# Two attention and two spectral layers on one core: the token transform written with real cosine and sine coefficients

## The chip, the core and the metric

The kernel runs on one core of a Trainium2 chip. The core has five engines with queues of their own that run in program order: TensorE (PE, with its weight loads as PEld), VectorE (DVE), ScalarE (ACT), GpSimd (POOL) and SyncE (SP, which here only issues DMAs). They meet through semaphores. The metric is the time of one launch on the device, in microseconds, and lower is better. Inputs and output are float32.

## The reference

```python
def _B_ref(x, w_r, w_i):
    B, S, D = x.shape                       # 1, 2048, 576
    X = rfft2(x, axes=(-2, -1))
    X = X * (w_r + 1j * w_i)                # 2048 x 289
    return irfft2(X, s=(S, D), axes=(-2, -1))

x = A_x
x = x + _A_ref(_layernorm(x), A_wqkv, A_wo)   # attention, 32 heads of 18, causal window of 256
x = x + _B_ref(_layernorm(x), B_w_r, B_w_i)   # global filter in frequency
x = x + _A_ref(_layernorm(x), A_wqkv, A_wo)
x = x + _B_ref(_layernorm(x), B_w_r, B_w_i)
return x
```

The change is in `_B_ref`: a two-dimensional real Fourier transform over 2048 tokens and 576 features, a product with a complex weight, and the way back.

## The kernel before

One program does the four layers in turn. `layer_a` is an attention layer (layer norm, projection to queries, keys and values, scores, softmax, values, output projection). At its end it calls `layer_b`, the spectral layer. Instructions run on each engine in the order in which the code lists them. No scheduler moves them, so an instruction that waits holds up everything behind it on its engine.

The 2048 tokens are written as 128 x 16: token index = 16 n1 + n2, with n2 from 0 to 15. `layer_b` has three stages, and the second and third are pipelines that `pipe` writes out: in each step t it calls every stage function once, in the listed order, for the item t minus the function's lag.

- **The f stage** handles one n2 (128 tokens) at a time. `f0` applies the layer norm and forms sums and differences of mirrored features, `f1` transposes them (PSUM tile `tp`, one buffer) and splits them into a high and a low part (`et`), `f2` does the feature transform by matmul (`pf`) and splits it (`yh`, `yl`), and `f3` does a transform over the 128 values of n1 (`pz`) with 12 matmuls, copies it to `ye` on DVE and writes it to the DRAM scratch `yd[0]`. The same loop finishes the output projection of the attention layer: `out.unit` does 28 matmuls (`ops`) and the residual, `out.sums` and `out.stats` the layer norm's statistics (L584 to L591), and `out.ahead` transposes the next rows (`tpo`, in the same PSUM buffer as `tp`) and splits them (L537 to L550). Every product is in float32r with a high and a low part.
- **The g stage** handles 16 groups of 8 frequencies. `g1m` does the transform over n2 (`p`), multiplies by the weight `w` on DVE and combines on POOL (`uv`, L302 and L303). `g2` does the inverse over n2 (`pq`) and writes to the scratch `yd[1]`. Both use plain float32 and half the array's rows or columns per matmul. It ends with the first loads of the next stage.
- **The i stage** handles one n2 at a time again, with `pipe(NT, [(0, ly), (4, i1), (5, i2), (2, i0)])`. `ly` loads one n2, `i0` splits it into a high and a low part (`z`, shown as `oroom`: ACT L346, DVE L347, ACT L348, DVE L349), `i1` does the inverse over n1 (`pi`, 18 matmuls) and splits it (`zh`, `zl`: ACT L368, DVE L369, ACT L370, DVE L371), and `i2` does the inverse feature transform (`po`, 16 matmuls) and adds the residual (ACT L389, DVE L390 and L391, POOL L392 and L393). In step t the order is thus i1 for t-4, i2 for t-5, i0 for t-2. In the first spectral layer the steps from t = 7 on also carry pieces of the next attention layer (`nxt`).

In time, the first spectral layer runs from about 475 us (with the end of the output projection) to 748 us: the f stage to 621, the g stage to 668, the i stage to 750. The second runs from 1217 us to the end: the f stage to 1361, the g stage to 1409, the i stage to 1492.

Of the kernel before, what the change touches and what calls it, by code (L numbers as in the profile page):

```python
# [16 lines left out]
DF = 289  # L17
NF = 290
# [7 lines left out]
def hl(x):  # L26
    h = r12(x)
    l = r12(np.asarray(x, np.float64) - h)
    return h.astype(np.float32), l.astype(np.float32)

def consts_b():
    n = np.arange(DF)[:, None].astype(np.int64)
    f = np.arange(DF)[None, :].astype(np.int64)
    ang = 2 * np.pi * ((n * f) % D) / D
    C = np.cos(ang)
    Sn = np.sin(ang)
    Sn[:, 0] = Sn[:, 288] = 0.0
# [22 lines left out]
    G = np.exp(-2j * np.pi * ((n1 * n1.T) % 128) / 128)  # L60

    k1 = ((2 * np.arange(4)[None, None] + np.arange(2)[:, None, None]) * 16 + np.arange(16)[None, :, None])
    def cplx(M, axis):

        return [np.stack(p, axis=axis) for p in ((M.real, M.imag), (-M.imag, M.real))]

    gc = np.zeros((128, 2, 2, 2, 128), np.float32)

    ga = np.zeros((16, 2, 4, 2, 2, 256), np.float32)
    for j in range(2):  # L70
        for c, m in enumerate(cplx(G[:, k1[j]], 3)):
            gc[:, 0, j, c], gc[:, 1, j, c] = hl(m.reshape(128, 128))
        for c, m in enumerate(cplx(G.conj()[k1[j]], 2)):
            ga[:, c, :, 0, j], ga[:, c, :, 1, j] = hl(m.reshape(16, 4, 256))
# [12 lines left out]
    return dict(dc=dc, ic=ic, fc=fc.reshape(128, 4096), gc=gc.reshape(128, 1024), ga=ga.reshape(128, 1024), m2=m2.reshape(128, 4096))

def lay_w(wr, wi):
    w = np.zeros((16, 128, 2, NF), np.float32)  # L90
    for c, a in enumerate((wr, wi)):

        b = a.reshape(16, 8, 16, DF)

        w[:, :, c, :DF] = b.reshape(16, 4, 2, 16, DF).transpose(3, 2, 1, 0, 4).reshape(16, 128, DF)
    return w.reshape(16, 128, 2 * NF)

def layer_b(tc, src, dst, dcs, gc, ident, rh, rl, out, ic_d, fc_d, ga_d, m2_d, w_d, dram, nxt, share):
# [8 lines left out]
    with ExitStack() as stack:  # L107
# [10 lines left out]
        ga = rh[:, 4248:5272].rearrange("p (a j c) -> p a j c", a=2, j=2)  # L118
        ic = rh[:, 5272:8752].rearrange("p (a f) -> p a f", f=NF)
        pairs = [rl[:, 1160 * k:1160 * k + 1160] for k in range(4)]  # L120
        yis, tws = [[rl[:, at + 580 * k:at + 580 * k + 580].rearrange("p (a f) -> p a f", f=NF) for k in range(n)] for at, n in ((4640, 4), (6960, 2))]
# [12 lines left out]
                for q in range(2):  # L134
                    xs[n2 + q] = x[:, q]

        fc = cp.tile([128, 16, 2, 2, 64], F32, name="fc")
        m2 = cp.tile([128, 16, 2, 128], F32, name="m2")
        eos = []
        for j in range(4):  # L140
            e = cp.tile([128, 2, 290], F32, name=f"eo{j}")
# [13 lines left out]
        def pre(n2):  # L155

            if n2 in (1, 4, 7, 10):
                k = (1, 4, 7, 10).index(n2)
                nc.sync.dma_start(fc[:, 4 * k:4 * k + 4].rearrange("p g j c m -> p (g j c m)"), fc_d[:, 1024 * k:1024 * k + 1024])
            if n2 in (2, 6, 9, 12):  # L160
                k = (2, 6, 9, 12).index(n2)
                nc.sync.dma_start(m2[:, 4 * k:4 * k + 4].rearrange("p g c m -> p (g c m)"), m2_d[:, 1024 * k:1024 * k + 1024])
            if n2 % 2 and n2 // 2 < NW:
                pre_w(n2 // 2)

# [43 lines left out]
        def f3(n2, h):  # L209
            pz = pp.tile([128, 2, 512], F32, tag="mm", name=f"pz{n2}", bufs=3)  # L210
            yh, yl = h["yh"], h["yl"]
            for j in range(2):
                ms = [(t, c, y) for c in range(2) for t, y in ((0, yh), (0, yl), (1, yh))]
                for k, (t, c, y) in enumerate(ms):
                    T.matmul(pz[:, j, 0:NF], gc[:, t, j, c], y[:, c], start=k == 0, stop=k == 5)  # L215
# [73 lines left out]
        def g1m(g, h):  # L289
            ps = pp.tile([128, 2, 512], F32, tag="mm", name=f"p2_{g}", bufs=3)  # L290

            for c in range(2):
                for j in range(2):
                    T.matmul(ps[64 * j:64 * j + 64, c, 0:NF], fc[:, g, j, c], h["y"][:, j], start=True, stop=True)  # L294
# [3 lines left out]
            V.tensor_mul(p1, ps[:, :, 0:NF], w)  # L298
# [3 lines left out]
            P.tensor_sub(uv[:, 0], p1[:, 0], p1[:, 1])  # L302
            P.tensor_add(uv[:, 1], p2[:, 0], p2[:, 1])  # L303
# [3 lines left out]
        def g2(g, h):  # L307
# [2 lines left out]

            for c in range(2):
                for j in range(2):
                    T.matmul(pq[:, j, 0:NF], m2[64 * j:64 * j + 64, g, c], uv[64 * j:64 * j + 64, c], start=c == 0, stop=c == 1)  # L313
# [29 lines left out]
        def i0(n2, h):  # L343
            z = zs[n2 % 3]
            zf = z.bitcast(F32)
            A.copy(z[:, 0, :, 0:DF], h["y"][:, :, 0:DF])  # L346
            V.tensor_sub(z[:, 1, :, 0:DF], h["y"][:, :, 0:DF], zf[:, 0, :, 0:DF])  # L347
            A.copy(z[:, 0, :, 320:353], zf[:, 0, :, 256:289])  # L348
            V.tensor_copy(z[:, 1, :, 320:353], zf[:, 1, :, 256:289])  # L349

        def i1(n2, h):
# [2 lines left out]
            psf = ps.rearrange("p a b -> p (a b)")  # L354
            for ch in range(3):
                lo, m = ((0, 128), (128, 128), (256, 97))[ch]
                o = psf[0:m, ch * 256:ch * 256 + 256]
                k = 0
                for c in range(2):
                    for sl, mo in ((0, ga[:, 0, c]), (0, ga[:, 1, c]), (1, ga[:, 0, c])):  # L360
                        T.matmul(o, z[:, sl, c, lo:lo + m], mo, start=k == 0, stop=k == 5)  # L361
# [115 lines left out]
class Out:  # L477
# [6 lines left out]
    def room(self):  # L484
# [5 lines left out]
        self.gc = rh[:, 9216:10240].rearrange("p (a j b c) -> p a j b c", a=2, j=2, b=2)  # L490
# [18 lines left out]
    def consts(self):  # L509

        self.dcs = []
        for k, t in enumerate(("wraw", "wraw", "wqh", "wqh", "wql")):
            d = self.bp.tile([128, 2, NF], F32R, tag=t, name=f"dc{k}", bufs=2)
            self.nc.sync.dma_start(d.bitcast(F32), self.dc_d[:, 2 * k:2 * k + 2].bitcast(F32))
            self.dcs.append(d)
        self.nc.sync.dma_start(self.gc.rearrange("p a j b c -> p (a j b c)").bitcast(F32), self.gc_d.bitcast(F32))

    def load(self, u):
        self.nc.sync.dma_start(self.o[u % 3], self.ov[:, u])
# [673 lines left out]
```

## Time and profile before

| | us |
|---|---|
| median of 3 runs (1497.03, 1502.33, 1503.27) | 1502.33 |
| the profiled execution's own time | 1494.12 |
| its span in the profile | 1492.4 |
| PE busy in the span | 1428.8 |
| DVE busy | 941.7 |
| ACT busy | 811.4 |
| POOL busy | 686.1 |

The busy time of PE counts pipelined matmuls whose ends are modelled, so two matmuls that follow each other overlap in it. In rows of the timeline the first two numbers are the start and the duration in microseconds, and a bracket at the end tells how long the engine had been idle and what it waited for. The start-to-start spacing of two rows on an engine is what one of them costs there. The windows view gives, for a stretch of time, its length and then the busy time of PE, PEld, DVE, ACT and POOL with the number of instructions, the granted TensorE clock as a share of full speed, the DMA share and GB/s.

### The profile page before, as it was taken

The numbers are of one execution on the slowest core, as the hardware profiler recorded it, in microseconds if no ns is written. First come the engines' busy times: TensorE is split into PE (matmuls) and PEld (weight loads), VectorE is DVE, ScalarE is ACT, GpSimd is POOL, SyncE is SP. The second block draws the span as 40 slices with busy tenths as digits, with TensorE's granted clock in tenths as the row PEclk, the third lists the DMA queues.
The fourth block names the chain that finished last, engine by engine and source line by source line (L and its number), as shares of the span: only waits on it lengthen the run. The fifth ranks groups of instructions, "written<-read, shape, count | busy, mean of one in ns | idle before, by whom it ended". The sixth has DMA issues, their size and how long they took to land.

```text
span 1492.4 us, 34861 instructions
## 1 busy us (share of the span) xinstructions
PE 1428.8 (96%) x12124; PEld 1091.4 (73%) x12124; DVE 941.7 (63%) x3090; ACT 811.4 (54%) x1962; POOL 686.1 (46%) x1124
## 2 busy tenths in 40 slices
PE   7999999999998899999999999999999988999997
PEld 7976666666656799759999756666665568997697
DVE  5328777777882655456852388777777735554476
ACT  5524777777785444224454257777777754442243
POOL 2266455555565432153421954555454644332434
PEclk9999999999999999999999999999999999999999
DMA  6656556565445465767663575555554354667663
GB/s 194 198 171 215 170 180 190 180 188 176 155 131 162 129 216 183 241 209 247 240 173 92 184 219 169 168 159 166 158 149 144 102 173 142 210 198 248 215 206 124
DMA packets 203241, 267.66 MB, mean 179 GB/s; under 512 B 103938, under 2 KB 109058, under 8 KB 202106
## 3 DMA queue, kind: packets, MB, share of 16 engines
q1 hardware_dynamic: 192890, 242.75, 52.9%
q10 hardware_dynamic: 7808, 15.62, 3.0%
q0 software_dynamic: 2368, 7.05, 1.7%
q8 instruction: 97, 1.59, 0.4%
q14 instruction: 78, 0.64, 0.1%
HBM read 166.71 MB, written 102.00 MB: 180 GB/s over the span
## 4 chain that ended last, share of the span: by engine, by line
PE 70%; DVE 6%; DMA 6%; ACT 5%; POOL 3%; issue 2%; SPq 1%; ACTq 0%; POOLq 0%; DVEq 0%
PE pj L798 16%; PE S L855 11%; PE U L912 10%; PE ops L555 6%; PE E L892 5%; PE vps L738 4%; PE pf L202 3%; PE pz L215 3%; PE pi L361 2%; DMA ofree<-yd 2%; PE tpo L926 2%; PE po L382 2%; ACT P L893 2%; PE pq L313 1%; PE p L294 1%
## 5 line engine op out<-in xcount | busy, mean ns | idle before, releaser
L857 DVE CUSTOM_DVE_ANT_0 jk<-S,mask 128x384 bf16<-128x384 f32 (+2 forms) x1024 | 490.6, 529 | 112.1 <-PE E L892 61.6
L893 ACT ACTIVATE P<-E 128x384 f32<-128x384 f32 (+2 forms) x1024 | 409.2, 476 | 124.0 <-PE E L892 104.2
L895 POOL TENSOR_SCALAR_AFFINE_SELECT P<-P 128x512 f32<-128x512 f32 x256 | 163.1, 637 | 276.7 <-ACT P L893 254.7
L855 PE MATMUL S<-ks,qs 63*128 63x384 f32 (+2 forms) x1024 | 269.7, 372 | 1.1 <-issue 0.4
L892 PE MATMUL E<-qs,ks 64*128 64x384 f32 (+2 forms) x1024 | 222.5, 373 | 5.5 <-ACT P L893 3.7
L855 PEld LDWEIGHTS S<-ks,qs 63*128 63x128 f32 x1024 | 140.9, 185 | 105.7 <-DVE m L857 73.7
L912 PE MATMUL U<-P,vq 128*19 128x128 f32 (+1 forms) x3840 | 188.5, 329 | 1.0 <-ACT us L917 1.0
L798 PE MATMUL pj<-xh,wqh 128*128 128x512 f32 x360 | 156.1, 433 | 2.9 <-ACT vt L742 1.7
L912 PEld LDWEIGHTS U<-P,vq 128*19 128x19 f32 x3840 | 95.8, 98 | 77.9 <-issue 21.4
L898 POOL TENSOR_SCALAR_AFFINE_SELECT P<-P 128x512 f32<-128x512 f32 x224 | 142.8, 637 | 0.0
L892 PEld LDWEIGHTS E<-qs,ks 64*128 64x128 f32 x1024 | 114.1, 185 | 19.8 <-ACT P L893 10.9
L555 PE MATMUL ops<-oroom 128*128 128x288 f32 x840 | 120.8, 299 | 4.4 <-DVE oroom L538 3.0
L798 PE MATMUL pj<-xh,wql 128*128 128x512 f32 x360 | 124.5, 419 | 0.4 <-POOL wql L460 0.4
L798 PE MATMUL pj<-xl,wqh 128*128 128x512 f32 x288 | 121.6, 422 | 0.0
L555 PEld LDWEIGHTS ops<-oroom 128*128 128x128 f32 x840 | 112.8, 189 | 6.2 <-DVE oroom L538 3.9
L171 POOL TENSOR_TENSOR eo<-xn 128x287 f32<-128x287 f32 x32 | 26.1, 816 | 153.7 <-ACT xn L169 127.0
L798 PEld LDWEIGHTS pj<-xh,wqh 128*128 128x128 f32 x360 | 67.6, 188 | 34.2 <-issue 10.4
L813 DVE TENSOR_TENSOR sg<-pj,sg 128x512 fp32r<-128x512 f32 x72 | 49.5, 687 | 58.3 <-ACT sg L810 58.2
L857 DVE DVE_READ_ACCUMULATOR2_ANT m<- 128x1 f32 x1024 | 85.1, 83 | 0.0
L361 PE MATMUL pi<-oroom 128*128 128x256 f32 (+1 forms) x576 | 77.4, 289 | 5.0 <-ACT oroom L346 3.8
L798 PEld LDWEIGHTS pj<-xh,wql 128*128 128x128 f32 x360 | 64.2, 189 | 21.0 <-issue 10.7
L361 PEld LDWEIGHTS pi<-oroom 128*128 128x128 f32 (+1 forms) x576 | 72.8, 186 | 6.9 <-ACT oroom L346 4.8
(179 smaller groups left out, 2626.6 us busy)
## 6 DMA issues: line engine op xcount, KB each, us to landing
qk_d<-sg SPq DMA_DIRECT2D x56, 512.0 KB
qs<-qk_d SPq DMA_DIRECT2D x384, 72.0 KB
ks<-qk_d SPq DMA_DIRECT2D x348, 72.0 KB
v_d<-vt SPq DMA_DIRECT2D x32, 304.0 KB
vq<-v_d SPq DMA_DIRECT2D x16, 608.0 KB
yd<-ye SPq DMA_DIRECT2D x32, 290.0 KB
wt<-in_w SPq DMA_DIRECT2D x16, 580.0 KB
x<-ofree SPq DMA_DIRECT2D x32, 288.0 KB
```

Source lines behind the costliest of these rows:

```text
L361: T.matmul(o, z[:, sl, c, lo:lo + m], mo, start=k == 0, stop=k == 5)
L555: self.nc.tensor.matmul(self.ps[u][n][:, 0:288], x, self.w[p][:, wk * D + n * 288:wk * D + n * 288 + 288], start=first and i == 0, stop=la ...
L738: T.matmul(ps[:, n, 0:288], xT(xk, c), w[:, wk, n * 288:(n + 1) * 288], start=i == 0, stop=i == len(ks) - 1)
L798: T.matmul(box["ps"].rearrange("r (n p) -> r n p", n=NT) if second else box["ps"], w[:, wk], x, start=s == 0, stop=s == len(ks) - 1)
L813: V.tensor_sub(rest[:, 1], by, rest[:, 0].bitcast(F32))
L855: T.matmul(ps[:, 0:N], q[b:b + 63, pair, i * 128:i * 128 + 128], k[b:b + 63, pair, lo:hi], start=True, stop=True)
L857: V.tensor_tensor_reduce(out=jk[:, 0:N], in0=ps[:, 0:N], in1=mask[:, 384 - N:384], scale=1.0, scalar=-3e38, op0=ALU.add, op1=ALU.max, accu ...
L892: T.matmul(ps[:, 0:nq], k[b:b + 64, pair, j * 128:j * 128 + 128], q[b:b + 64, pair, j * 128:j * 128 + nq], start=True, stop=True)
L893: A.activation(p[:, hl_, 0:nq], ps[:, 0:nq], AF.Exp, scale=SC)
L895: P.affine_select(out=p[:, :, 0:128], in_=p[:, :, 0:128], pattern=[[0, 4], [1, 128]], compare_op=ALU.is_ge, fill=0.0, base=0, channel_mult ...
L898: P.affine_select(out=p[:, :, 256:384], in_=p[:, :, 256:384], pattern=[[0, 4], [-1, 128]], compare_op=ALU.is_gt, fill=0.0, base=0, channel ...
L912: T.matmul(U[32 * h:32 * h + 19, (q0 % 4) * 128:(q0 % 4) * 128 + 128 * (q1 - q0)], vts[n][:, j, h], pt[n, j][:, h, (q0 - j) * 128:(q1 - j) ...
```

## The change

The transform over n1 is no longer complex. Its input is real for each of the cosine and sine parts of the features, so the coefficients over n1 are taken as cosines and sines of 64 frequencies, and a frequency k is kept together with its mirror 128 - k. The constants `gc` and `ga` are half as large, `fc` and `m2` are 17 groups instead of 16, and the rows of `w` follow the new order.

- In `f3` the 12 matmuls become 6: for j = 1 and then j = 0, three each. DVE's one copy `ye` becomes three instructions: ACT copies half of the PSUM tile to `half`, and DVE writes the sum and the difference of the other half and `half`.
- In `g1m` the group g = 0 has 8 matmuls instead of 4 (each output accumulates two), and in `g2` the 4 matmuls of group 0 contract over 128 rows instead of 64.
- In `i0` POOL first writes the sum and the difference of the two loaded halves to a new tile `both` (two buffers), and ACT's copy and DVE's subtraction read `both` in place of the loaded tile.
- In `i1` there are still 18 matmuls, but each has 128 columns instead of 256 and writes a range of its own.

```diff
         def f3(n2, h):
...
-            for j in range(2):
-                ms = [(t, c, y) for c in range(2) for t, y in ((0, yh), (0, yl), (1, yh))]
-                for k, (t, c, y) in enumerate(ms):
-                    T.matmul(pz[:, j, 0:NF], gc[:, t, j, c], y[:, c], start=k == 0, stop=k == 5)
+            for j in (1, 0):
+                for k, (t, y) in enumerate(((0, yh), (0, yl), (1, yh))):
+                    T.matmul(pz[:, j, 0:NF], gc[:, t, j], y[:, j], start=k == 0, stop=k == 2)
             ye = wp.tile([128, 2, NF], F32, tag="ye", name=f"ye{n2}", bufs=3)
-            V.tensor_copy(ye, pz[:, :, 0:NF])
+            half = ip.tile([128, 2, NF], F32, tag="both", name=f"half{n2}", bufs=2)[:, 0]
+            A.copy(half, pz[:, 1, 0:NF])
+            V.tensor_add(ye[:, 0], pz[:, 0, 0:NF], half)
+            V.tensor_sub(ye[:, 1], pz[:, 0, 0:NF], half)
...
         def g1m(g, h):
...
-                    T.matmul(ps[64 * j:64 * j + 64, c, 0:NF], fc[:, g, j, c], h["y"][:, j], start=True, stop=True)
+                    T.matmul(ps[64 * j:64 * j + 64, c, 0:NF], fc[:, g, j, c], h["y"][:, j], start=True, stop=g > 0)
+                    if g == 0:
+                        T.matmul(ps[64 * j:64 * j + 64, c, 0:NF], fc[:, 16, j, c], h["y"][:, 1 - j], start=False, stop=True)
...
         def g2(g, h):
...
-                    T.matmul(pq[:, j, 0:NF], m2[64 * j:64 * j + 64, g, c], uv[64 * j:64 * j + 64, c], start=c == 0, stop=c == 1)
+                    r = slice(64 * j, 64 * j + 64) if g else slice(0, 128)
+                    T.matmul(pq[:, j, 0:NF], m2[r, g if g or j == 0 else 16, c], uv[r, c], start=c == 0, stop=c == 1)
...
         def i0(n2, h):
             z = zs[n2 % 3]
             zf = z.bitcast(F32)
-            A.copy(z[:, 0, :, 0:DF], h["y"][:, :, 0:DF])
-            V.tensor_sub(z[:, 1, :, 0:DF], h["y"][:, :, 0:DF], zf[:, 0, :, 0:DF])
+            y = h["y"]
+            w = ip.tile([128, 2, NF], F32, tag="both", name=f"both{n2}", bufs=2)
+            P.tensor_add(w[:, 0, 0:DF], y[:, 0, 0:DF], y[:, 1, 0:DF])
+            P.tensor_sub(w[:, 1, 0:DF], y[:, 0, 0:DF], y[:, 1, 0:DF])
+            A.copy(z[:, 0, :, 0:DF], w[:, :, 0:DF])
+            V.tensor_sub(z[:, 1, :, 0:DF], w[:, :, 0:DF], zf[:, 0, :, 0:DF])
             A.copy(z[:, 0, :, 320:353], zf[:, 0, :, 256:289])
             V.tensor_copy(z[:, 1, :, 320:353], zf[:, 1, :, 256:289])
...
         def i1(n2, h):
...
-                o = psf[0:m, ch * 256:ch * 256 + 256]
-                k = 0
                 for c in range(2):
-                    for sl, mo in ((0, ga[:, 0, c]), (0, ga[:, 1, c]), (1, ga[:, 0, c])):
-                        T.matmul(o, z[:, sl, c, lo:lo + m], mo, start=k == 0, stop=k == 5)
-                        k += 1
+                    o = psf[0:m, ch * 256 + 128 * c:ch * 256 + 128 * c + 128]
+                    for k, (sl, mo) in enumerate(((0, ga[:, 0, c]), (0, ga[:, 1, c]), (1, ga[:, 0, c]))):
+                        T.matmul(o, z[:, sl, c, lo:lo + m], mo, start=k == 0, stop=k == 2)
```

The rest of the diff builds the new constants on the host (`consts_b`, `pairs_of`, `lay_w`), makes the tiles `fc`, `m2`, `gc` and `ga` fit, and loads one more group with the last pieces of `fc` and `m2`.

More of the change, by code (lines that the diff above doesn't have):

```diff
@@ L59, in consts_b @@
     n1 = np.arange(128)[:, None]
-    G = np.exp(-2j * np.pi * ((n1 * n1.T) % 128) / 128)
-    k1 = ((2 * np.arange(4)[None, None] + np.arange(2)[:, None, None]) * 16 + np.arange(16)[None, :, None])
-    def cplx(M, axis):
-        return [np.stack(p, axis=axis) for p in ((M.real, M.imag), (-M.imag, M.real))]
-    gc = np.zeros((128, 2, 2, 2, 128), np.float32)
-    ga = np.zeros((16, 2, 4, 2, 2, 256), np.float32)
-    for j in range(2):
[L71 to L74, printed above, removed]
+    m = np.arange(64)
+    wave = np.exp(2j * np.pi * ((n1 * m) % 128) / 128)
+    sign = 1.0 - 2.0 * (n1 % 2)
+    up, down = (np.concatenate([e, z[:, 1:]], axis=1) for e, z in ((np.ones((128, 1)), wave.real), (0 * sign, wave.imag)))
+    even = np.stack([up, -down], axis=2)
+    odd = np.stack([down, up], axis=2)
+    even[:, 0] = odd[:, 0] = np.concatenate([np.ones((128, 1)), sign], axis=1)
+    even, odd = [a.reshape(128, 16, 4, 2) for a in (even, odd)]
+    gc = np.zeros((128, 2, 2, 128), np.float32)
+    ga = np.zeros((16, 2, 4, 2, 2, 128), np.float32)
+    for j, a in enumerate((even, odd)):
+        gc[:, 0, j], gc[:, 1, j] = hl(a.reshape(128, 128))
+        back = a.copy()
+        back[:, 0, 0] *= 0.5
+        ga[:, :, :, 0, j], ga[:, :, :, 1, j] = hl(back.transpose(1, 3, 2, 0))
+    k1 = pairs_of()
+    def cplx(M, axis):
+        return np.stack((M.real, M.imag), axis=axis)
     fc = np.zeros((16, 4, 2, 16, 2, 2, 4, 16), np.float32)
+    fx = np.zeros((16, 4, 2, 2, 2, 4, 16), np.float32)
     m2 = np.zeros((2, 4, 16, 16, 2, 2, 4, 16), np.float32)
+    mx = np.zeros((2, 4, 16, 2, 2, 2, 4, 16), np.float32)
     for j in range(2):
@@ L91, in lay_w @@
     for c, a in enumerate((wr, wi)):
-        b = a.reshape(16, 8, 16, DF)
-        w[:, :, c, :DF] = b.reshape(16, 4, 2, 16, DF).transpose(3, 2, 1, 0, 4).reshape(16, 128, DF)
+        k = pairs_of()[..., None] + 128 * np.arange(16)
+        w[:, :, c, :DF] = a[k].transpose(1, 0, 2, 3, 4).reshape(16, 128, DF)
     return w.reshape(16, 128, 2 * NF)
@@ L135, in ld @@
                     xs[n2 + q] = x[:, q]
-        fc = cp.tile([128, 16, 2, 2, 64], F32, name="fc")
-        m2 = cp.tile([128, 16, 2, 128], F32, name="m2")
+        fc = cp.tile([128, 17, 2, 2, 64], F32, name="fc")
+        m2 = cp.tile([128, 17, 2, 128], F32, name="m2")
         eos = []
@@ L489, in room @@
         self.oL = [rh[:, 8448 + 256 * k:8704 + 256 * k] for k in range(3)]
-        self.gc = rh[:, 9216:10240].rearrange("p (a j b c) -> p a j b c", a=2, j=2, b=2)
+        self.gc = rh[:, 9216:9728].rearrange("p (a j c) -> p a j c", a=2, j=2)
         small = f[:, 8130:8170]
```

40 lines of the change are left out of this document (29 added, 11 removed).

## The prediction

> **What bounds the kernel now.** I read the engine totals first, then the busy time per stretch in the spectral stages, and then the timeline of each engine through one turn of each loop that the change touches.
>
> ```profile
> PE 1428.8 (96%) x12124; PEld 1091.4 (73%) x12124; DVE 941.7 (63%) x3090; ACT 811.4 (54%) x1962; POOL 686.1 (46%) x1124
> ```
>
> ```profile
> 1426.47:1477.80 51.33, 51.33 (x411) 51.33 (x410) 43.09 (x72) 23.52 (x60) 23.61 (x24) 1.00 0.57 186
> 519.70:587.20 67.50, 67.50 (x523) 67.50 (x521) 38.35 (x96) 28.92 (x64) 22.02 (x54) 1.00 0.63 200
> ```
>
> PE looks like the bound: it never rests in twelve turns of the second i stage (first row) or in eight turns of the first f stage (second row, 67.5 / 8 = 8.44 us each). But DVE is busy for 43.1 of 51.3 us in the i stage, and a share cannot tell whether its gaps are free. So I followed one turn there, from one residual add (DVE L390) to the next:
>
> ```profile
> 1436.21 0.46 DVE L390 TENSOR_TENSOR xo<-ofree,po 128x289 f32<-128x289 f32 x1
> 1436.58 0.45 DVE L391 TENSOR_TENSOR xo<-ofree,po 128x287 f32<-128x287 f32 x1
> 1436.95 1.22 DVE L347 TENSOR_TENSOR oroom<-ofree,oroom 128x578 fp32r<-128x578 f32 x1
> 1438.97 0.69 DVE L369 TENSOR_TENSOR zl<-pi,zh 128x512 fp32r<-128x512 f32 x1 [0.20 <-ACT zh L368]
> 1440.11 0.43 DVE L371 TENSOR_TENSOR zh<-pi,zh 33x256 fp32r<-33x256 f32 x1 [0.44 <-ACT zh L370]
> 1440.57 0.46 DVE L390 TENSOR_TENSOR xo<-ofree,po 128x289 f32<-128x289 f32 x1
> ...
> 1438.20 0.25 ACT L348 CAST oroom<-oroom 128x66 fp32r<-128x66 f32 x1 [1.61 <-DVE oroom L347]
> 1438.36 0.58 ACT L368 CAST zh<-pi 128x512 fp32r<-128x512 f32 x1
> 1439.70 0.38 ACT L370 CAST zh<-pi 97x256 fp32r<-97x256 f32 x1 [0.76 <-DVE zl L369]
> ...
> 1436.75 0.81 POOL L392 TENSOR_TENSOR xo<-xo,bs 128x289 f32<-128x289 f32 x1 [2.38 <-DVE xo L390]
> 1437.51 1.21 POOL L393 TENSOR_TENSOR xo<-xo,bs 128x287 f32<-128x287 f32 x1
> ```
>
> Each start follows the end before it: L390, L391, L347 on DVE; then ACT L348, which waits for L347; L368 behind it on ACT; DVE L369; ACT L370; DVE L371; DVE L390 of the next turn. The spacings are 0.37 + 0.37 + 1.25 + 0.16 + 0.61 + 0.73 + 0.41 + 0.46 = 4.36 us. That is a closed ring through two in-order engines, as long as PE's turn (51.33 / 12 = 4.28 us). POOL is outside it: L392 and L393 hang on it, and nothing on it waits for them.
>
> **The i stage after the change.** In step t, `pipe` calls i2 ahead of i0. On POOL the two new instructions (the sum and difference for item t-2) therefore stand behind L392 and L393 of item t-5, and those wait for DVE's residual add. ACT's copy of `z` needs the new tile, DVE's L347 needs that copy, and the ring goes on from L347 as before. So POOL's four instructions and ACT's copy now lie in the ring. What they cost, undisturbed:
>
> ```profile
> 1419.29 0.67 ACT L346 CAST oroom<-ofree 128x578 fp32r<-128x578 f32 x1 [3.52 <-DMA ofree<-yd]
> 1419.99 0.76 DVE L347 TENSOR_TENSOR oroom<-ofree,oroom 128x578 fp32r<-128x578 f32 x1 [3.76 <-ACT oroom L346]
> 1420.79 0.25 ACT L348 CAST oroom<-oroom 128x66 fp32r<-128x66 f32 x1 [0.83 <-DVE oroom L347]
> ...
> 1481.07 0.69 POOL L393 TENSOR_TENSOR xo<-xo,bs 128x287 f32<-128x287 f32 x1
> ```
>
> ```profile
> L302 POOL TENSOR_TENSOR uv<-ofree 128x290 f32<-128x290 f32 x32 | 22.4, 700 | 75.4 <-DVE ofree L298 75.4
> L303 POOL TENSOR_TENSOR uv<-p 128x290 f32<-128x290 f32 x32 | 22.3, 698 | 1.0
> ```
>
> L347 takes 0.76 us alone against 1.22 beside POOL's L393, and L393 0.69 against 1.21. In the new ring they follow one another, so both take their short time. The new instructions have the shape of L302 and L303, 0.70 us. The new turn, start to start: L390 to L392 0.54, L392 0.76, L393 0.66, sum 0.67, difference and hand-over 0.75, ACT's copy to L347 0.70, L347 to L348 0.80, then 0.16 + 0.61 + 0.73 + 0.41 + 0.46 as now. That is 7.25 us, **2.89 us more in each turn**.
>
> ```profile
> 1423.14 0.46 DVE L390 TENSOR_TENSOR xo<-ofree,po 128x289 f32<-128x289 f32 x1
> 1479.76 0.46 DVE L390 TENSOR_TENSOR xo<-ofree,po 128x289 f32<-128x289 f32 x1
> ...
> 683.02 0.46 DVE L390 TENSOR_TENSOR xo<-ofree,po 128x289 f32<-128x289 f32 x1
> 742.48 0.46 DVE L390 TENSOR_TENSOR xo<-ofree,po 128x289 f32<-128x289 f32 x1
> ```
>
> Items 3 to 15 pass i0 while a residual add is ahead of them: 13 turns. In the second layer these two rows are 56.62 us apart, 13 x 4.36. There the change costs 13 x 2.89 = 37.6, and 1.4 more because the start (ACT L346 at 1419.29, waiting for the load) now has two POOL instructions behind that load: 39.0. In the first layer the 13 turns take 59.46 us, with 2.8 us of the next layer's statistics among them, of which I keep half: 13 x 7.25 + 1.4 - 59.46 + 1.4 = 37.6. Together **+76.6**. Bounds: the new POOL instructions at 0.64 (L393 alone, less overlap) or 1.21 each (beside DVE), so -3 to +28.
>
> The narrower matmuls of `pi` buy nothing. PE's turn is 4.28 us with `pi` as it is, and at best 18 x 0.06 = 1.1 us shorter were each to take half its 0.12; either way it waits for a ring of 7.25.
>
> **The f stage.** Six matmuls of 0.135 us fewer, 0.81 us per turn, if PE alone sets the loop.
>
> ```profile
> 552.65 0.27 PE L185 MATMUL tp<-ident,eo 128*128 128x128 f32 x1
> 553.23 0.38 PE L215 MATMUL pz<-yh,oroom 128*128 128x290 f32 x1
> 554.93 0.97 PE L202 MATMUL pf<-dc,et 128*128 128x290 f32 x6
> ...
> 553.51 0.59 ACT L190 CAST et<-tp 128x512 fp32r<-128x512 f32 x1 [1.98 <-PE tp L187]
> 555.82 0.29 ACT L586 ACTIVATE ofree<-ofree,eps 128x1 f32<-128x1 f32 x1 [0.60 <-DVE ofree L585]
> ...
> 551.56 0.29 DVE L550 TENSOR_TENSOR oroom<-tpo,oroom 128x128 fp32r<-128x128 f32 x1 [0.33 <-ACT oroom L549]
> ...
> 554.12 0.69 DVE L191 TENSOR_TENSOR et<-tp,et 128x512 fp32r<-128x512 f32 x1 [0.45 <-ACT et L190]
> ...
> 556.34 0.15 DVE L590 RECIPROCAL ofree<-ofree 128x1 f32<-128x1 f32 x1
> ...
> L389 ACT COPY bs<-po 128x290 f32<-128x290 f32 x32 | 13.0, 407 | 3.8 <-PE po L386 3.8
> ```
>
> Two things take that gain. First, `pz` is what PE does while ACT and DVE make `et`. DVE's part of it (L191) ends at 554.81. With six matmuls fewer `pf` starts at 554.12, does the two matmuls that need only ACT's part, and would do the third at 554.39; it waits 0.42 us. So PE's turn becomes 8.44 - 0.81 + 0.42 = 8.05. Second, the single copy `ye` (done on DVE while ACT took the square root) becomes a row of three: ACT's `half` behind the root, about 556.0, 0.41 us (as L389, same shape, from PSUM), then two DVE instructions at the 0.37 spacing of L390 and L391. The reciprocal behind them starts at about 557.25 instead of 556.34, 0.91 us later, and with it `xn`, `yh` (behind `xn` on ACT), `yl`, and the split of `tpo`. That split now ends at 551.85 and frees the PSUM buffer 0.80 us before the next `tp` takes it at 552.65. The chain from one `tp` to the next is thus 8.44 - 0.80 + 0.91 = 8.55: it outlasts PE's 8.05, and PE's 8.44 now. **The loop gains nothing**, 11 turns x 0.11 = +1 per layer. At the end of the stage, with no output projection left, some of five saved 0.81 remain; I take 2 of 4 us. Both layers: -2. Bounds: -26 (32 x 0.81, nothing waits) to +6 (nothing left at the end, 0.2 more per turn).
>
> **The g stage.**
>
> ```profile
> 627.36 1.49 PE L313 MATMUL pq<-uv,m 64*128 64x290 f32 x8 [0.55 <-POOL uv L302]
> 629.35 1.20 PE L294 MATMUL p<-ofree,fc 128*64 128x290 f32 x8 [0.50 <-DMA ofree<-yd]
> 630.47 1.25 PE L313 MATMUL pq<-uv,m 64*128 64x290 f32 x8
> ```
>
> Four float32 matmuls (eight records) of a group take 1.12 to 1.2 us. Group 0 has four more in `p`, +1.1, and its `pq` loses the halves that run side by side, which costs 0 to 1.2 more. 0.5 of it falls into the wait for the load at 629.35. I take 1.5 per layer: **+3**, bounds 1 to 5. The smaller constants and their DMAs lie under 8 us turns of PE and count nothing; if that cover were gone they would still be shorter than now.
>
> **Sum.** 76.6 - 2 + 3 = 77.6, say +77. The profiled execution took 1494.12 us, 1.7 of it around its span, so 1571 on that basis; the median of the runs is 1502.33, 0.5% above it, and I forecast from it: **1579 us**.
>
> **The rivals.**
>
> *PE decides, and it is faster.* i0 runs two steps ahead of i1, and if that hides POOL's work and the split of `tpo` still comes before the next `tp`, the f stage gives its 26 us and the i stage stays at the 4.36 of its old ring: 1502 - 26 + 3 = 1479. For it: PE shows no idle time in either loop. It decides from the point at which the f chain's extra is under the 0.80 us of slack (I find 0.91) and POOL's pair stands ahead of L392 in its queue (it stands behind). Chance 0.04.
>
> *The change does not do what it says.* Nothing in `pi` is saved, the f gain is lost as above, and POOL's pair is hidden: 1502 + 3 - 2 = 1503. It needs the same open ring. Chance 0.04.
>
> *PE at half clock.* In a turn of 7.25 us PE would work for 3.2 to 4.28 and rest for 3 to 4.
>
> ```profile
> 1420.01 0.50 PE L361 MATMUL pi<-oroom 128*128 128x256 f32 x2 [1.76 <-ACT oroom L346]
> ...
> 1422.00:1423.00 1.00, 1.00 (x7) 1.00 (x7) 0.56 (x2) 0.72 (x3) 0.00 (x0) 0.50 0.47 185
> ```
>
> After a rest of only 1.76 us the granted clock fell to 0.50. Were it halved throughout, PE's turn would be 6.4 to 8.5 us, and at 8.5 it would outlast the ring by 1.3 in 26 turns: 1579 + 33 = 1612. Against it: at half clock PE is busy all the time, and it got its full clock back within 4 us of work. Chance 0.05. By the Trainium skill (TensorE: Matmul & The Clock Gate, section "HAM oscillation — how this bites in real kernels") only PE rests beyond some 3.4 us cost the clock, which would leave this rival nothing where each rest is shorter; the trace shows a halving after less, so the rule alone doesn't exclude it.
>
> *POOL and DVE meet more often than I think.* If the new pair takes 1.21 each, as L393 does beside L347, the turn is 8.3: 1579 + 27 = 1606. Nothing on DVE with SBUF inputs is due at that time. Chance 0.07.
>
> **How the numbers follow.** My forecast has 0.80 and is the predicted time. Its own range is 1560 to 1592 (0.35 us per turn in 26 turns, 5 for the other stages, 3 for the base). To leave out no more than 2 in 10 I go to 1553 below (part of the f gain kept) and 1602 above (part of the last two rivals). 0.5% is about what a measurement of this kernel can tell from no change. Slower by more: 0.80 + 0.05 + 0.07 = 0.92; within: 0.04; faster: 0.04.
>
> **What would show it.** Right: spacings of DVE L426 (the old L390) near 7.25 us in both i stages, ACT's copy into `z` released by POOL, PE idle for 3 us per turn there; in the f loop a turn still near 8.5 us, `tp` released by DVE's last split, and fewer `pz` records. Wrong: an i turn under 5 us, or an f turn near 7.6. If the i turn is 8 or more, the clock column and the lengths of POOL's four rows tell which of the last two rivals it is.

## The result, and the profile after

| | before | after |
|---|---|---|
| median, runs side by side | 1499.99 us (4 runs, 1497.03 to 1503.27) | 1575.15 us (4 runs, 1572.13 to 1576.38) |
| profiled execution, and its span | 1494.12, 1492.4 | 1574.53, 1572.4 |
| ratio, 95% interval | | 1.0497 [1.0466, 1.0529] |

The changed kernel is slower by 75.2 us, with 176 PE instructions fewer. The page's engine totals:

```profile
PE 1464.7 (93%) x11948; PEld 1108.7 (71%) x11948; DVE 927.3 (59%) x3122; ACT 823.9 (52%) x1994; POOL 715.2 (45%) x1188
```

PE's busy time grew with fewer instructions. The windows view shows where: the 13 turns of each i stage, cut from the first residual add (DVE L426, the old L390) to the last one in the ring (second layer, then first).

```profile
1466.05:1559.55 93.50, 77.36 (x456) 72.76 (x455) 37.67 (x79) 27.32 (x66) 35.88 (x52) 0.78 0.32 105
687.95:782.65 94.70, 77.16 (x456) 72.45 (x455) 40.48 (x90) 27.80 (x68) 37.48 (x55) 0.78 0.45 154
```

Before, these stretches took 56.62 and 59.46 us (the residual adds in the prediction). They are longer by 36.88 and 35.24, together 72.1 us; the medians differ by 75.2 and the two profiled executions by 80.4. A turn is 93.50 / 13 = 7.19 us. In the second layer PE now rests for 16 of 93.5 us where it had rested for none, and part of its work runs at half clock (0.78 on average), so its busy time per matmul rose. No engine is busy throughout: what sets the pace is a chain. One turn in the second layer, with DVE, ACT and POOL one after the other:

```profile
1516.42 0.46 DVE L426 TENSOR_TENSOR xo<-ofree,po 128x289 f32<-128x289 f32 x1
...
1520.45 0.76 DVE L385 TENSOR_TENSOR oroom<-both,oroom 128x578 fp32r<-128x578 f32 x1 [3.21 <-ACT oroom L384]
...
1522.01 0.69 DVE L405 TENSOR_TENSOR zl<-pi,zh 128x512 fp32r<-128x512 f32 x1 [0.57 <-ACT zh L404]
1523.14 0.43 DVE L407 TENSOR_TENSOR zh<-pi,zh 33x256 fp32r<-33x256 f32 x1 [0.44 <-ACT zh L406]
1523.60 0.46 DVE L426 TENSOR_TENSOR xo<-ofree,po 128x289 f32<-128x289 f32 x1
...
1519.74 0.68 ACT L384 CAST oroom<-both 128x578 fp32r<-128x578 f32 x1 [3.51 <-POOL both L383]
1521.24 0.25 ACT L386 CAST oroom<-oroom 128x66 fp32r<-128x66 f32 x1 [0.83 <-DVE oroom L385]
1521.40 0.58 ACT L404 CAST zh<-pi 128x512 fp32r<-128x512 f32 x1
1522.74 0.37 ACT L406 CAST zh<-pi 97x256 fp32r<-97x256 f32 x1 [0.76 <-DVE zl L405]
...
1516.95 0.81 POOL L428 TENSOR_TENSOR xo<-xo,bs 128x289 f32<-128x289 f32 x1 [4.43 <-DVE xo L426]
1517.71 0.70 POOL L429 TENSOR_TENSOR xo<-xo,bs 128x287 f32<-128x287 f32 x1
1518.37 0.69 POOL L382 TENSOR_TENSOR both<-ofree 128x289 f32<-128x289 f32 x1
1519.02 0.69 POOL L383 TENSOR_TENSOR both<-ofree 128x289 f32<-128x289 f32 x1
```

The baton goes DVE L426, POOL L428, L429, L382, L383, ACT L384, DVE L385, ACT L386 and L404, DVE L405, ACT L406, DVE L407, DVE L426. Each member starts where the one before ends, POOL's four take 2.79 us from the first start to the hand-over, and the 3.5 us for which ACT waits and the 3.2 for which DVE waits are the same stretch seen from two engines.

In the f stage the turn is 8.60 us where it was 8.44. One turn of the changed kernel, PE first (its output projection left out), then ACT and DVE:

```profile
553.47 0.33 PE L214 MATMUL tp<-ident,eo 128*128 128x128 f32 x1 [0.16 <-DVE oroom L586]
...
555.75 0.81 PE L231 MATMUL pf<-dc,et 128*128 128x290 f32 x4 [0.19 <-DVE et L220]
...
562.07 0.33 PE L214 MATMUL tp<-ident,eo 128*128 128x128 f32 x1 [0.17 <-DVE oroom L586]
...
556.90 0.38 ACT L246 COPY half<-pz 128x290 f32<-128x290 f32 x1
...
557.32 0.46 DVE L247 TENSOR_TENSOR ye<-pz,half 128x290 f32<-128x290 f32 x1 [0.65 <-ACT half L246]
557.69 0.45 DVE L248 TENSOR_TENSOR ye<-pz,half 128x290 f32<-128x290 f32 x1
558.06 0.15 DVE L626 RECIPROCAL ofree<-ofree 128x1 f32<-128x1 f32 x1
...
561.73 0.29 DVE L586 TENSOR_TENSOR oroom<-tpo,oroom 128x128 fp32r<-128x128 f32 x1 [0.33 <-ACT oroom L585]
```

Both waits that the prediction named are there: PE's third `pf` waits for DVE's part of `et`, and the next `tp` waits for DVE's last split of `tpo` (L586, the old L550), which did not wait for anything before. The reciprocal stands behind `half`, the sum and the difference.

### The profile page after: what moved, and what is told of

It reads as the page before. It is cut to its first block, busy times and chain, and to the rows that moved or that the text cites. A ratio compares the mean times of both kernels' runs of the same rounds, so it can differ in the third digit from the quotient of the medians.

```text
span 1572.4 us, 34592 instructions
## 1 busy us (share of the span) xinstructions
PE 1464.7 (93%) x11948; PEld 1108.7 (71%) x11948; DVE 927.3 (59%) x3122; ACT 823.9 (52%) x1994; POOL 715.2 (45%) x1188
## 5 line engine op out<-in xcount | busy, mean ns | idle before, releaser
L948 PEld LDWEIGHTS U<-P,vq 128*19 128x19 f32 x3840 | 95.8, 98 | 77.6 <-issue 21.5
L398 PE MATMUL pi<-oroom 128*128 128x128 f32 (+1 forms) x576 | 89.5, 316 | 29.4 <-ACT oroom L384 21.7
L398 PEld LDWEIGHTS pi<-oroom 128*128 128x128 f32 (+1 forms) x576 | 83.2, 230 | 37.4 <-ACT oroom L384 26.1
L385 DVE TENSOR_TENSOR oroom<-both,oroom 128x578 fp32r<-128x578 f32 x32 | 25.2, 788 | 109.0 <-ACT oroom L384 109.0
L428 POOL TENSOR_TENSOR xo<-xo,bs 128x289 f32<-128x289 f32 x32 | 25.8, 807 | 130.2 <-DVE xo L426 126.3
```

The lines of the kernel that those rows point to most:

```text
L385: V.tensor_sub(z[:, 1, :, 0:DF], w[:, :, 0:DF], zf[:, 0, :, 0:DF])
L948: T.matmul(U[32 * h:32 * h + 19, (q0 % 4) * 128:(q0 % 4) * 128 + 128 * (q1 - q0)], vts[n][:, j, h], pt[n, j][:, h, (q0 - j) * 128:(q1 - j) ...
```

## The experiments

**1. POOL's pair one step earlier.** The only edit to the changed kernel:

```diff
-        def i0(n2, h):
+        def i0a(n2, h):
...
-            w = ip.tile([128, 2, NF], F32, tag="both", name=f"both{n2}", bufs=2)
+            w = h["w"] = ip.tile([128, 2, NF], F32, tag="both", name=f"both{n2}", bufs=2)
             P.tensor_add(w[:, 0, 0:DF], y[:, 0, 0:DF], y[:, 1, 0:DF])
             P.tensor_sub(w[:, 1, 0:DF], y[:, 0, 0:DF], y[:, 1, 0:DF])
+
+        def i0(n2, h):
+            z = zs[n2 % 3]
+            zf = z.bitcast(F32)
+            w = h["w"]
...
-        pipe(NT, [(0, ly), (4, i1), (5, i2), (2, i0)], ...)
+        pipe(NT, [(0, ly), (5, i1), (6, i2), (3, i0), (2, i0a)], ...)
```

> The changed kernel with POOL's pair in a stage function of its own, one step ahead of ACT's copy into z (lags: load 0, pair 2, copy and split 3, i1 5, i2 6). The instructions are the same, the pair still stands behind the residual instructions on POOL, but ACT's copy takes the pair of the step before. Theory (the ring through POOL, ACT and DVE): the long chain now has two turns to go round, 7.2 / 2 = 3.6 us, so the old ring of DVE and ACT decides again, 4.36 us or up to 4.9 with POOL and DVE meeting more: 26 turns x 2.3 to 2.8 back, 5 us for the longer pipeline: 1507 to 1520 us. Rival (POOL's extra work costs its time wherever it stands): turn 7.2, 1575 to 1585 us. Rival (narrow matmuls on a throttled PE set the turn): 7.2, 1575 us.

Measured: 1503.32 us (10 runs), ratio to the kernel before 1.000 [0.998, 1.002]; the 13 turns of the second layer take 4.35 to 4.37 us each. The instructions are those of the changed kernel; their order alone gives back 72 us. DVE, ACT and POOL in one turn (L429 is the residual add, L387 ACT's copy, L388 DVE's subtraction, L380 and L381 POOL's pair):

```profile
1454.94 0.46 DVE L429 TENSOR_TENSOR xo<-ofree,po 128x289 f32<-128x289 f32 x1
...
1455.67 1.23 DVE L388 TENSOR_TENSOR oroom<-both,oroom 128x578 fp32r<-128x578 f32 x1
...
1454.63 0.69 ACT L387 CAST oroom<-both 128x578 fp32r<-128x578 f32 x1
...
1455.47 0.81 POOL L431 TENSOR_TENSOR xo<-xo,bs 128x289 f32<-128x289 f32 x1 [1.07 <-DVE xo L429]
1456.24 1.21 POOL L432 TENSOR_TENSOR xo<-xo,bs 128x287 f32<-128x287 f32 x1
1457.41 0.69 POOL L380 TENSOR_TENSOR both<-ofree 128x289 f32<-128x289 f32 x1
1458.06 0.69 POOL L381 TENSOR_TENSOR both<-ofree 128x289 f32<-128x289 f32 x1
```

POOL's pair still stands behind the residual, but it now works for the next step, and ACT's copy at 1454.63 has not waited for anything. The ring is the old one. The time is 4 us under the expected range, since I had allowed the turn up to half a microsecond over the old one.

**2. The pair on DVE instead of POOL.** In `i0` of the changed kernel:

```diff
-            P.tensor_add(w[:, 0, 0:DF], y[:, 0, 0:DF], y[:, 1, 0:DF])
-            P.tensor_sub(w[:, 1, 0:DF], y[:, 0, 0:DF], y[:, 1, 0:DF])
+            V.tensor_add(w[:, 0, 0:DF], y[:, 0, 0:DF], y[:, 1, 0:DF])
+            V.tensor_sub(w[:, 1, 0:DF], y[:, 0, 0:DF], y[:, 1, 0:DF])
```

> The changed kernel with the sum and the difference in i0 on DVE instead of POOL. Theory (ring): POOL leaves the ring and two DVE instructions at 0.37 spacing enter it: L426 0.37, L427 0.37, pair 0.75, ACT's copy 0.75, then 0.80 + 0.16 + 0.61 + 0.73 + 0.41 + 0.46 = 5.4 us per turn, up to 5.9 where the residual's POOL instructions meet DVE's: 1528 to 1541 us. Rival (narrow matmuls or PE's clock set the turn): 7.2 as before, 1575 us. Rival (DVE is the bound, so more work on it is slower): above 7.2, over 1580 us.

Measured: 1557.75 us (one run), turn 6.42: a miss in size. The same addition at the start of the stage, with nothing on POOL, then two rows of DVE in the ring and the one of POOL beside them:

```profile
1446.25 0.46 DVE L382 TENSOR_TENSOR both<-ofree 128x289 f32<-128x289 f32 x1 [8.62 <-DMA ofree<-ze]
...
1479.84 0.93 DVE L382 TENSOR_TENSOR both<-ofree 128x289 f32<-128x289 f32 x1
...
1480.41 0.91 POOL L429 TENSOR_TENSOR xo<-xo,bs 128x287 f32<-128x287 f32 x1
1480.69 0.95 DVE L383 TENSOR_TENSOR both<-ofree 128x289 f32<-128x289 f32 x1
```

DVE's additions of two SBUF inputs take 0.93 and 0.95 us beside POOL's residual and 0.46 without it, so it is the meeting that makes them long. The two cost 1.83 in the ring (1479.84 to 1481.67, where ACT's copy starts), about 1.0 over what I had expected of them, and 5.4 + 1.0 is the turn measured. The ring theory stands (the pair is still in it), its price on DVE does not.

**3. The kernel before with POOL's pair alone.** Nothing of the new transform is in it; POOL passes the two loaded halves on through an addition of zeros:

```diff
-            A.copy(z[:, 0, :, 0:DF], h["y"][:, :, 0:DF])
-            V.tensor_sub(z[:, 1, :, 0:DF], h["y"][:, :, 0:DF], zf[:, 0, :, 0:DF])
+            w = ip.tile([128, 2, NF], F32, tag="both", name=f"both{n2}", bufs=2)
+            P.tensor_add(w[:, 0, 0:DF], y[:, 0, 0:DF], zero[:, 0:DF])
+            P.tensor_add(w[:, 1, 0:DF], y[:, 1, 0:DF], zero[:, 0:DF])
+            A.copy(z[:, 0, :, 0:DF], w[:, :, 0:DF])
+            V.tensor_sub(z[:, 1, :, 0:DF], w[:, :, 0:DF], zf[:, 0, :, 0:DF])
```

> The kernel before with nothing of the change but POOL's pair: i0 adds a zero tile to each of the two loaded halves on POOL, and ACT and DVE read the sums. Theory (ring): turn 7.2 us in both i stages, 26 x 2.84 + 3 us: about 1577 us. Rival (narrow matmuls or PE's clock): they aren't in this kernel, so 1500 us. Rival (half the loss is in the f and g stages): about 1540 us.

Measured: 1577.67 us (one run), turn 7.30. Here are ACT's copy and two residual adds of DVE:

```profile
1517.87 0.46 DVE L397 TENSOR_TENSOR xo<-ofree,po 128x289 f32<-128x289 f32 x1
...
1521.31 0.67 ACT L353 CAST oroom<-both 128x578 fp32r<-128x578 f32 x1 [3.63 <-POOL both L352]
...
1525.16 0.46 DVE L397 TENSOR_TENSOR xo<-ofree,po 128x289 f32<-128x289 f32 x1
```

A loss of the same size (75 us) comes with two POOL instructions in that place, and without any other part of the change. The turn is 0.11 longer than in the changed kernel; POOL's first addition takes 0.80 us here, 0.69 there.

**4. Every `pi` accumulation run twice.** Does PE, at its lower clock, set the turn?

```diff
-                    for k, (sl, mo) in enumerate(((0, ga[:, 0, c]), (0, ga[:, 1, c]), (1, ga[:, 0, c]))):
-                        T.matmul(o, z[:, sl, c, lo:lo + m], mo, start=k == 0, stop=k == 2)
+                    for k, (sl, mo) in enumerate(2 * ((0, ga[:, 0, c]), (0, ga[:, 1, c]), (1, ga[:, 0, c]))):
+                        T.matmul(o, z[:, sl, c, lo:lo + m], mo, start=k % 3 == 0, stop=k % 3 == 2)
```

> The changed kernel with every accumulation of pi run twice, the second run starting anew over the first: 18 more matmuls of 128 columns per turn, about 1.9 us of PE. Theory (ring without PE): PE's turn grows from 4.1 to 6.0 us and stays under 7.2: turn 7.2, 1572 to 1580 us. Rival (PE decides, at a lower clock): turn 9.1, about 1625 us.

Measured: 1589.86 us (one run). The windows view of the 13 turns of the second layer, and the first work of PE in that stage:

```profile
1480.56:1574.03 93.47, 85.85 (x695) 82.09 (x694) 37.66 (x78) 27.16 (x65) 35.85 (x52) 0.96 0.32 105
```

```profile
1464.04 12.90 PE L398 MATMUL pi<-oroom 128*128 128x128 f32 x70 [0.78 <-DVE oroom L385]
```

The turn stays at 7.19 us with 18 more matmuls in it, and with more to do PE gets a mean clock of 0.96 instead of 0.78: the low clock of the changed kernel costs nothing in the turns. The total is 10 us above the expected range. Most of that lies ahead of the turns, where I had not looked for it: from ACT's last copy of the g stage to the first residual add it takes 29.03 and 27.47 us in the two layers, where the changed kernel takes 22.03 and 21.13, 13.3 us more together. Before the ring closes, PE is on the path, and there the work of `pi` is doubled (70 matmuls in 12.90 us here, 34 in 6.92 in the changed kernel).

**5. The sum and difference of the f stage behind the split of `tpo`.** In the changed kernel `f3` is cut in two, its matmuls (`f3m`) and the rest (`f3e`: `half`, `ye` and the store):

```diff
             if t > 1:
-                f3(t - 1, hs[t - 1])
+                f3m(t - 1, hs[t - 1])
             f0(u, hs[u])
             f2(t, hs[t])
             out.ahead(u + 2, pp)
+            f3e(t - 1, hs[t - 1])
```

> The changed kernel with the eviction of pz (ACT's half, DVE's sum and difference, the write to DRAM) called at the end of each turn of the f loop, behind the split of tpo, instead of ahead of the layer norm's reciprocal. Same instructions, i stage untouched. Theory (the chain tp, et, statistics, half, ye, reciprocal, xn, yh, split of tpo, next tp sets the f turn at 8.60): the chain falls back to 7.6 to 7.7 and PE decides, with its wait for et: 8.05 to 8.15 us per turn, about 21 turns x 0.5: 1562 to 1566 us. Rival (PE sets the turn and the f stage has its whole gain already): turn stays 8.6, 1575 us. Rival (the wait for et isn't there): 7.63, about 1555 us.

Measured: 1568.48 us (4 runs), ratio to the kernel before 1.0426 [1.0389, 1.0463], 6.7 under the changed kernel's median (its ratio was 1.0497). In the profile the two f stages, from the first to the last `et`, are 9.0 us shorter together. The turn fell from 8.60 to 8.22, not to the 8.05 to 8.15 expected. PE in one turn (`tp` at 558.50 now follows without a wait), and DVE's last split with the sum behind it:

```profile
551.77 0.53 PE L231 MATMUL pf<-dc,et 128*128 128x290 f32 x2
552.50 0.81 PE L231 MATMUL pf<-dc,et 128*128 128x290 f32 x4 [0.19 <-DVE et L220]
...
558.50 0.27 PE L214 MATMUL tp<-ident,eo 128*128 128x128 f32 x1
...
557.45 0.29 DVE L595 TENSOR_TENSOR oroom<-tpo,oroom 128x128 fp32r<-128x128 f32 x1 [0.33 <-ACT oroom L594]
557.75 0.46 DVE L251 TENSOR_TENSOR ye<-pz,half 128x290 f32<-128x290 f32 x1
```

With the chain out of the way PE decides, and its own loss to `et` shows: the first two `pf` take 0.73 us to the start of the third (551.77 to 552.50) where 0.27 is the pace without a wait. That is 0.46 lost in the wait, and the `pf` part as a whole is 0.58 longer than before. With that term the prediction's 8.44 - 0.81 + 0.42 = 8.05 becomes 8.21.

**6. The kernel before with the new eviction and the old 12 matmuls.** DVE's one copy becomes `half`, sum and difference:

```diff
-            V.tensor_copy(ye, pz[:, :, 0:NF])
+            half = ip.tile([128, 2, NF], F32, tag="both", name=f"half{n2}", bufs=2)[:, 0]
+            A.copy(half, pz[:, 1, 0:NF])
+            V.tensor_add(ye[:, 0], pz[:, 0, 0:NF], half)
+            V.tensor_sub(ye[:, 1], pz[:, 0, 0:NF], half)
```

> The kernel before with nothing of the change but the longer eviction of pz: ACT copies a half, DVE writes sum and difference (so what goes on from there is not the transform). The 12 matmuls stay. Theory (the f turn is a chain through ACT and DVE, not PE): 8.6 us per turn as in the changed kernel, 0.16 more than 8.44: about 1504 us. Rival (matmul time and eviction add up): 8.6 + 0.8 = 9.4, 1521 us. Rival (PE decides, the eviction is hidden): 8.44, 1500 us.

Measured: 1507.65 us (one run), f turn 8.59 to 8.61. With 12 matmuls in `pz` or with 6, the turn is 8.60. The eviction, not PE, sets the f loop in both.

**7. Experiments 1 and 5 together.**

> The changed kernel with both moves, POOL's pair one step earlier (as in e1) and the late eviction of pz (as in e3). Theory (two separate rings, each opened): the gains add up, 1503 - 10 to 13: 1490 to 1494 us, under the kernel before by about 0.6%. Rival (the DMA or the end of the f stage takes the f gain back): 1500 to 1504 us.

Measured: 1495.41 us (11 runs), ratio 0.9935 [0.9913, 0.9957]. Run again with the next two kernels beside it:

> The same kernel as e4_both, timed beside e9_warm on one chip. Expected as before: 0.9935 of the kernel before, within 0.002.

Measured: 1492.88 us (8 runs), ratio 0.9948 [0.9923, 0.9973]. So the new transform does make a faster kernel than the one before, by 0.5 to 0.65%, once its two new pieces of work stand where nothing waits for them. Where these 8 to 9 us lie, no profile shows. The span of the same code was 1495.0 in one profile and 1490.7 in the other, and the profiled execution of before (1494.12) was faster than every other execution of it (lowest 1495.11). Against that profile the f stages of the second run are 4.0 us shorter, but the g stages are 0.8 and the starts of the i stages 5.2 longer.

**8. As 7, with `i0` ahead of `i2`.** The idea was to take DVE's subtraction and ACT's copy out from behind the residual add.

```diff
-        pipe(NT, [(0, ly), (5, i1), (6, i2), (3, i0), (2, i0a)], ...)
+        pipe(NT, [(0, ly), (5, i1), (3, i0), (6, i2), (2, i0a)], ...)
```

> As e4, and in the steps of the i stage the split of z (i0) stands ahead of the residual (i2) on ACT and DVE. Theory (the i turn of 4.36 is DVE's and ACT's ring, with L385 at 1.23 us because it meets POOL's residual): DVE's row is i1, split, residual, so POOL's residual runs beside DVE's instructions from PSUM; the ring falls to 3.5 to 3.9 us and PE decides, 18 x 0.108 + 16 x 0.133 = 4.08 us: 26 turns x 0.25 less than e4, 1483 to 1488 us. Rival (POOL's pair now meets the split, or POOL's queue becomes the ring): 4.36 or more, 1490 us and above.

Measured: 1518.63 us (6 runs), ratio 1.0096 [1.0063, 1.013]; the turn is 5.41. The theory fell. One turn on DVE, POOL and ACT, and two rows of PE:

```profile
1472.85 0.46 DVE L438 TENSOR_TENSOR xo<-ofree,po 128x289 f32<-128x289 f32 x1 [0.38 <-ACT bs L437]
...
1476.88 0.76 DVE L397 TENSOR_TENSOR oroom<-both,oroom 128x578 fp32r<-128x578 f32 x1 [1.74 <-ACT oroom L396]
...
1478.25 0.46 DVE L438 TENSOR_TENSOR xo<-ofree,po 128x289 f32<-128x289 f32 x1 [0.39 <-ACT bs L437]
...
1473.39 0.80 POOL L440 TENSOR_TENSOR xo<-xo,bs 128x289 f32<-128x289 f32 x1 [2.66 <-DVE xo L438]
...
1475.44 0.69 POOL L390 TENSOR_TENSOR both<-ofree 128x289 f32<-128x289 f32 x1
...
1476.17 0.68 ACT L396 CAST oroom<-both 128x578 fp32r<-128x578 f32 x1 [1.49 <-POOL both L390]
...
1477.83 0.39 ACT L437 COPY bs<-po 128x290 f32<-128x290 f32 x1
...
1473.82 2.04 PE L410 MATMUL pi<-oroom 128*128 128x128 f32 x18 [1.15 <-DVE xo L439]
...
1477.62 0.43 PE L434 MATMUL po<-oroom,zh 97*128 97x290 f32 x2
```

The ring is POOL's again. DVE's residual add (L438) releases POOL's residual (L440, L441), the pair (L389, L390) stands behind it, ACT's copy (L396) waits for the pair, DVE's subtraction (L397) for the copy, and ACT's `bs` (L437) and the next residual add now stand behind these two. The spacings are 0.54 + 2.78 + 0.71 + 0.95 + 0.42 = 5.40 us. In experiments 1 and 7 the copy of a step stands behind the residual of that step, so the same chain has two turns to go round; with `i0` ahead of `i2` it has one. PE rests too: `pi` and `po` share three PSUM buffers, and `pi` waits 1.15 us in each turn for the one that the residual add gives back. But PE is not in the ring: its last `po` of this turn ends at 1478.05, and ACT's `bs` for that item starts only at 1483.23. This is read from the trace; no further run tests it.

**9. As 7, with 62 matmuls in `warm` ahead of the i stage instead of 50.** The idea was to keep PE's clock up over the wait for the first load.

> As e4_both, with 62 instead of 50 matmuls on constants between the g and the i stage (warm), so that PE works on until POOL's pair and ACT's copy have brought the first z. Theory (the new 1.9 us rest of PE there halves the clock for the first pi and po matmuls): from ACT's last copy of the g stage to the first residual add in the second layer falls from 20.9 us to about 19.3 (as in the kernel before), 3 us for both layers: about 0.2% under e4_both. Rival (the start is longer for POOL's pair alone, PE's clock hides): 20.9 stays, no difference.

Measured: 1494.58 us (12 runs), ratio 0.9952 [0.9932, 0.9973], no difference from the second run of experiment 7. The first `pi` of the second layer, and the next one:

```profile
1415.69 3.70 PE L410 MATMUL pi<-oroom 128*128 128x128 f32 x34 [0.77 <-DVE oroom L397]
...
1423.86 0.44 PE L410 MATMUL pi<-oroom 128*128 128x128 f32 x2 [2.27 <-ACT oroom L396]
```

The 34 matmuls take 3.70 us instead of 6.92 in the second run of experiment 7, so the clock was kept. But then PE stands 2.27 us for ACT's copy of the third item, which came 17.70 us behind the last copy of the g stage (16.43 in that run), and the next 16 `pi` matmuls take 3.01 us: the half clock came back one item later. The start of the second layer took 22.0 us, where 19.3 were expected and 21.3 were taken in that run. In the first layer it took 21.0 instead of 22.3, but two of the next turns became 4.79 and 7.41 us, with DVE's residual add behind PE's `po`. The rest was moved, not removed.

## Why the prediction was right

**The i turn.** Right, and in size: 7.25 us were summed, 7.19 measured; 76.6 us for both i stages, and 36.88 + 35.24 for the turns with 1.86 + 2.88 for the starts make 76.9. The step it rests on, that POOL's pair stands behind L392 and L393 and ACT's copy behind the pair, is shown by experiments 1 (same instructions, other order, the loss gone) and 3 (the pair alone, the loss as large). That all of POOL's and DVE's rows would take their short times held as well: 0.81, 0.70, 0.69, 0.69 and 0.76. One sign did not come as written: PE rests for 1.2 us in a turn and not for 3, since part of its work ran at half clock.

**The start of the i stage** cost 1.9 us in the second layer and 2.9 in the first, where I had 1.4. The pair behind the load costs 1.38 in both. The rest is PE, which the prediction left out of the start. The first residual add of the first layer:

```profile
687.95 0.46 DVE L426 TENSOR_TENSOR xo<-ofree,po 128x289 f32<-128x289 f32 x1 [1.62 <-ACT bs L425]
...
687.52 0.40 ACT L425 COPY bs<-po 128x290 f32<-128x290 f32 x1 [1.64 <-PE po L422]
```

After a rest of 2.88 us (1.88 in the second layer) PE does the first 34 `pi` matmuls in 6.92 us (4.27 before, with twice the columns), and the add, which had waited for nothing, waits for its `po`. In the ring it starts 0.46 us behind DVE L407; here it starts 1.58 us later than that, and 0.90 in the second layer. The load landed 0.08 and 0.43 us earlier: 1.38 + 1.58 - 0.08 = 2.88 and 1.38 + 0.90 - 0.43 = 1.85.

**"PE's matmuls buy nothing."** Right in the turns. Each `pi` did not take half its time either: 18 of 128 columns take 1.97 us (experiment 1's ring), 18 of 256 took 2.28 before.

```profile
1457.27 1.97 PE L401 MATMUL pi<-oroom 128*128 128x128 f32 x18
```

**The f loop.** Right in mechanism: the chain sets it (8.60 measured, 8.55 summed, and 8.60 in experiment 6 with the old matmuls). Mis-sized were five terms. The chain's turn is 0.16 longer than before, not 0.11: the sum left out the 0.05 us from the end of DVE's last split (562.02) to the `tp` that it releases (562.07). The loop has 8 turns of that length in each layer, not 11. The wait for `et` is worth 0.58 instead of 0.42, which only shows once the chain is out of the way (experiment 5). The first turn of the loop became 0.55 us longer (12.15 to 12.7), which I had not counted. And the 2 us that I kept for the end of the stage did not come: behind the loop one turn gained 0.2, the next lost 0.84, and the others moved by -0.5 to +1.4 with no sum of one sign. From the first to the last `et` of the stage it is +1.6 us in the first layer and +3.5 in the second, so +5.1 where I had -2.

**The g stage.** +0.8 and +0.9 us where I had 1.5 each: group 0's additional `p` delays the first product with the weight by 0.7 us in the first layer and 0.6 in the second, and the rest lies beside other work. Its `pq`, with 128 rows in each matmul instead of 64, took 2.22 us where it had taken 1.49 (the first of the g rows in the prediction). The row of the first layer:

```profile
629.34 2.22 PE L347 MATMUL pq<-uv,m 128*128 128x290 f32 x8 [0.66 <-POOL uv L335]
```

**The sum.** 76.9 + 5.1 + 1.7 = 83.7. The unchanged attention layer between the two spectral layers was 3.5 us shorter in this execution, which no part of the change explains, and the two profiled executions differ by 80.4. Against the 77.6 summed, f brought 7 more and g 1.3 less. The medians differ by 75.2, because the profiled execution of before lay 5.9 under its median and that of after 0.6 under its own: the base and the attention layer took up what the f step had missed. That the forecast of 1579 comes within 4 us of 1575.15 is luck in these terms; the i turn is not.

**The rivals.** "PE decides, and it is faster" needed the pair ahead of the residual in POOL's queue and the f eviction inside its slack; neither held. Experiment 7 gets what the two would give (the pair works a step ahead, the eviction stands behind the split), and then the sign turns (0.9935 [0.9913, 0.9957]). Not to the 1479 of that rival, though: an f turn gives 0.22 us (8.44 to 8.22) and not 0.81, and the i stages still start later than before. "It doesn't do what it says" fell with POOL's rows. "PE at half clock" was right about the clock and wrong about the price: experiment 4 shows that PE had the time to spend in the turns, and the two starts cost 1.58 and 0.90 us. By the rule of the Trainium skill that was cited beside that rival (TensorE: Matmul & The Clock Gate, section "HAM oscillation — how this bites in real kernels"), rests of this length should not have cost the clock at all; the 0.78 of the turns, with 1.2 us of rest in each, goes against it here. "POOL and DVE meet more often" did not happen on POOL, but its price was seen in experiment 2, where the pair was put on DVE.

## What to carry to other kernels

In a loop over in-order engines, look for the ring: from one instruction of a turn to the same one of the next, by waits and by places in the queues. An instruction put on an idle engine is free only if it does not stand between two members of the ring; the same two instructions cost 72 us in one place and nothing one step earlier. Count also how many turns a chain has to go round: experiment 1 gave it one more by issuing the pair a step earlier, and experiment 8 took that back by moving a single stage function. And an eviction that is one instruction longer delays everything behind it in its queue, so it goes behind what the next matmul waits for.

## What the runs showed of the hardware

Half the columns saved 14% of the time of the 18 `pi` matmuls of an item: 1.97 us with 128 columns and 2.28 with 256, each matmul with a weight load of its own. Six of the 18 load 97 columns of weights instead of 128. Start to start, in the row at 1457.27, the matmuls that load 128 are 0.112 us apart and those that load 97 are 0.086; with 256 columns (before, at 1426.47) both are 0.118 apart. So the load sets the pace of the narrow ones. By the Trainium skill (TensorE: Matmul & The Clock Gate, section "LDWEIGHTS (loading the stationary operand)") a load of P columns costs P / 1.2 ns, an estimate of 107 ns for 128 columns and 81 for 97; the trace agrees within 5 ns, with that as the floor under a matmul with its load.

A DVE instruction with two SBUF inputs and a POOL instruction beside it lengthen each other: 1.23 and 1.21 us in experiment 1, 0.76 and 0.70 for the same two in the changed kernel, where they don't meet. That is half a microsecond on each, in records of both engines. The rows read as if the later one stood until the earlier was nearly through: DVE L388 starts 0.61 us before POOL's L431 ends and is 0.47 longer, L432 starts 0.66 before L388 ends and is 0.51 longer, and in experiment 2 L383 starts 0.63 before L429 ends and is 0.50 longer. Read so, POOL's L392 also had a part in the old ring, through the 0.46 us that L347 was longer there, though the prediction has POOL outside it.

PE's clock fell to 0.50 after a rest of 1.76 us at the start of the i stage (the rows stand in the prediction), and not after one of 0.64 (experiment 9). It was 0.78 on average in a loop in which PE rested for 16 of 93 us, and 0.96 with 18 more matmuls in the turn. But in experiment 3 PE rested for 25 of 95 us in that loop (second layer), and the clock was 0.94. So the length of the rest alone does not order these; what does, no run here shows.
